# Attention by groups of four heads over all queries, and the MLP at the end: reordering a tuned transformer-block kernel

## The chip, the cores and the metric

The kernel runs on one core of one Trainium2 chip. The metric is the device time of one execution in microseconds (us). A run is called slow if it is over 1.5% above the fastest of the same kernel; all comparisons below use fast runs only. Profiles are of one execution each.

Engines are named as in the profile: PE is TensorE (matmul), PEld its weight load (it overlaps PE), ACT is ScalarE, DVE is VectorE, POOL is GpSimd, SP is SyncE, whose queue (SPq) only issues DMAs here. SBUF and PSUM are the two memories in which the kernel keeps its tiles; it has matmuls write their results to PSUM. "L657" is line 657 of the kernel in question; line numbers of different kernels are not comparable.

## The reference

A block on 2048 tokens of width 640: attention of 32 heads (width 128) against a given cache of 2048 keys and values, then an MLP with a token shift. Both branches are modulated and gated by vectors computed from `c`.

```python
mod = (_silu(c) @ w_mod)                      # six vectors: sa ca ga sb cb gb
h = _layernorm(x) * (1 + ca) + sa
x = x + ga * attention(h, k_cache, v_cache, wq, wo)   # q = h @ wq, softmax over 2048 keys, @ wo
h = _layernorm(x) * (1 + cb) + sb
# _B_ref(h):
g  = _gelu(_layernorm(h) @ w1)                # 640 -> 640; quarters shifted by +1, -1, +2, -2 tokens
x1 = h + shifted(g) @ w2                      # 640 -> 640
h2 = _gelu(_layernorm(x1) @ w3) @ w4          # 640 -> 1728 -> 640
x = x + gb * (x1 + h2)
```

## The kernel before

Both kernels record all work as operations with a *planned* duration, a priority and the tiles read and written. A small list scheduler in the kernel simulates the engines with these durations and so fixes, before anything runs, the order of instructions of each engine. Semaphore waits follow from the tiles. A planned duration costs nothing on the chip, but it decides what stands behind what in an engine's queue.

```python
# choice of the scheduler in before: of what can start within 30 ns, the lowest priority number
    lim = min(st)[0] + 30.0
    c = min((x for x in st if x[0] <= lim), key=lambda x: x[1:3])
```

Before works chunk by chunk. For each of four chunks of 512 queries it runs through all 32 heads, so a *step* is one chunk and one head, and there are 128 steps. K, V and the query weights are loaded anew in each step.

```python
def step(ch, h):                              # s = ch * 32 + h
    dma("SP", ... e.dma_start_transpose(k.ap..., A_k_cache[0, h]) ...)     # K transposed by DMA
    dma("POOL", ... A_wq[:, h*128:(h+1)*128] ...)
    dma("POOL", ... A_v_cache[0, h] ...)
    P.op("PE", qp, KT * MM(QC), ...)          # query projection: 5 matmuls of 512 columns
    for j in range(NKT // 2):                 # 8 slots a step, each of 256 keys
        P.op("PE", smm, 2 * MM(QC), ..., s + j / 8 - 1.0)           # scores: 2 matmuls of 512 columns
        last_exp[s, j] = P.op("ACT", ... ACT.Exp ..., 1040, (sp,), (pt,), s + j / 8, ...)
        for b in range(2):
            P.op("PE", pv, 4 * 59, (pt, v), (o[b],), s + j / 8 - 0.9 + b * 0.01, accum=True)  # values
    # ... divide by the row sums on DVE into On
def wo_group(ch, g): ...                      # after each 4 heads: transpose On by DMA, project, add to y
def phase_b(ch): ...                          # MLP of chunk ch, run during the heads of chunk ch + 1
```

The elementwise work ahead of the MLP is all on DVE, two fused instructions a tile for the modulation; the inverse standard deviation comes from two tiny ACT instructions (Ln, then Exp with scale -0.5):

```python
    P.op("DVE", ... e.scalar_tensor_tensor(out=w.ap, in0=src, scalar=mvt[:, 0:1], in1=mod_t[pc][:],
                                           op0=ALU.subtract, op1=ALU.mult) ...)
    P.op("DVE", ... e.scalar_tensor_tensor(out=dst, in0=w.ap, scalar=rst.ap, in1=mod_t[pb][:],
                                           op0=ALU.mult, op1=ALU.add) ...)
```

Of the kernel before, what the change touches and what calls it, by code (L numbers as in the profile page):

```python
# [7 lines left out]
ACT = mybir.ActivationFunctionType  # L8
# [5 lines left out]
class Op:  # L14

    def __init__(self, eng, fn, dur, lat, prio, dma, kb):
        self.eng, self.fn, self.dur, self.lat, self.prio, self.dma, self.kb = eng, fn, dur, lat, prio, dma, kb
        self.deps = {}
        self.order = set()
        self.newps = None  # L20
        self.ptiles = ()
        self.succ = []
        self.ready = 0.0
        self.needed = False
        self.sem = self.semval = self.prev_dma = None
# [15 lines left out]
class Plan:  # L41
# [5 lines left out]
    def __init__(self):  # L47
        self.ops = []
        self.pools = {}

    def op(self, eng, fn, dur, reads=(), writes=(), prio=0.0, lat=80, dma=False, kb=0, after=(), accum=False):
        o = Op(eng, fn, dur, lat, prio, dma, kb)
# [23 lines left out]
        o.order.update(after)  # L76
        self.ops.append(o)
        return o

    def schedule(self):  # L80
        for o in self.ops:
            o.order = {d() if callable(d) else d for d in o.order}
            pre = set(o.deps) | o.order
            for d in pre:
                d.succ.append(o)
            o.ndep = len(pre)
# [7 lines left out]
        free = {p: [(0.0, b, ()) for b in range(len(bk))] for p, bk in self.pools.items()}  # L94
        left = {o.newps: len(o.newps.refs) for o in self.ops if o.newps is not None}
        self.busy = {e: 0.0 for e in self.ENG}
        self.all = []
        while len(self.all) < len(self.ops):
            best = None
            for e in self.ENG:  # L100
                st = []
                for o in avail[e]:
                    r = o.ready
# [10 lines left out]
                if best is None or c[0] < best[0]:  # L114
                    best = c
            s, o = best[0], best[3]
            e = o.eng
            avail[e].remove(o)
            if o.newps is not None:
# [16 lines left out]
            self.all.append(o)  # L136
            for u in o.succ:
# [14 lines left out]
    def emit(self, nc, es, ndma):  # L152
# [21 lines left out]
        for o in self.ops:  # L174
            for d, raw in o.deps.items():
                if waits_on(o, d, raw):
                    d.needed = True
# [9 lines left out]
        for o in self.all:  # L187
            kn = know[o.eng]
            w = {}
            ds = [d for d, raw in o.deps.items() if waits_on(o, d, raw)]  # L190
# [42 lines left out]


def fast_path(nc, es, flag, A_x, A_k_cache, A_v_cache, A_wq, A_wo, B_w1, B_w2, B_w3, B_w4, c, w_mod, out):
# [6 lines left out]
    FL = FF - (NF - 1) * 128  # L242
    G4 = D // 4
    HG = 4
    SCALE = float(DH) ** -0.5
# [8 lines left out]
    T = lambda ap: Tile(ap)  # L254

    def ring(name, n, shape, dt):
        return [T(sb("%s%d" % (name, i), shape, dt)[:]) for i in range(n)]

    S_ps = [ps("S%d" % i, [128, 1024]) for i in range(2)]
    O_ps = [ps("O%d" % i, [128, 512]) for i in range(2)]  # L260
    M_ps = [ps("M%d" % i, [128, 512]) for i in range(2)]
    P.pools = {"S": [t[:] for t in S_ps], "O0": [O_ps[0][:]], "O1": [O_ps[1][:]], "M": [t[:] for t in M_ps]}

    ident_t = sb("ident", [128, 128], BF16)
    ident = T(ident_t[:])
    ones = T(sb("ones", [128, 128], BF16)[:])
    mod = [[T(None), T(None)] for _ in range(6)]
    mod_t = [sb("mod%d" % i, [128, D], F32) for i in range(6)]
    rl_t = sb("rl", [128, 4 * NC * H], F32)
    rl = T(rl_t[:])  # L270
    WA_t = sb("WA", [128, NF * D], BF16)
    WB_t = sb("WB", [128, KT * FF], BF16)
    WA, WB = T(WA_t[:]), T(WB_t[:])
    small = lambda name, w, dt=F32: T(sb(name, [128, w], dt)[:])

    MM = lambda n: n / 2.4 + 3
    dve = lambda n, psum=False: (n + (150 if psum else 90)) / 0.96
    act = lambda n: (n + 230) / 1.2

    def dma(eng, fn, kb, reads, writes, prio):  # L280
        return P.op(eng, fn, 60 if eng == "SP" else 1000, reads, writes, prio, dma=True, kb=kb)

    P.op("POOL", lambda e: e.memset(ident_t[:], 0.0), 200, (), (ident,), -100)
    P.op("POOL", lambda e: e.affine_select(out=ident_t[:], in_=ident_t[:], pattern=[[-1, 128]], compare_op=ALU.not_equal,
                                           fill=1.0, base=0, channel_multiplier=1), 300, (ident,), (ident,), -100)
    P.op("POOL", lambda e: e.memset(ones.ap, 1.0), 200, (), (ones,), -50)

    EXPSET = "natural_log_exp_and_others"
    P.op("ACT", lambda e: e.preload_act_table_set(EXPSET), 1300, (), (), -200)

    def back_to_exp(g, prio):
        o = P.op("ACT", lambda e: e.preload_act_table_set(EXPSET), 1300, (), (), prio, after=tuple(g))
        return (o,)

    c_sb, c_e, c_f = small("c_sb", KT, BF16), small("c_e", KT), small("c_f", KT)
    s_bc = T(sb("s_bc", [128, KT, 128], BF16)[:])

    def ld_c(e):
        with nc.allow_non_contiguous_dma(reason="tiny c vector"):
            return e.dma_start(c_sb.ap, c[0].rearrange("(kt p) -> p kt", p=128))  # L300
    dma("SP", ld_c, 2, (), (c_sb,), -100)

    xin = ring("xin", 3, [128, D], BF16)
    n_x = [0]

    def load_x(j, prio):
        t = xin[n_x[0] % 3]
        n_x[0] += 1
        dma("SP", lambda e: e.dma_start(t.ap, x2d[j * 128:(j + 1) * 128, :]), 160, (), (t,), prio)
        return t  # L310

    first_x = [load_x(j, -99 + j) for j in range(2)]

    P.op("ACT", lambda e: e.activation(c_e.ap, c_sb.ap, ACT.Exp, scale=-1.0), 300, (c_sb,), (c_e,), -90)
    P.op("DVE", lambda e: e.tensor_scalar_add(out=c_e.ap, in0=c_e.ap, scalar1=1.0), 100, (c_e,), (c_e,), -90)
    P.op("DVE", lambda e: e.reciprocal(c_e.ap, c_e.ap), 150, (c_e,), (c_e,), -90)
    P.op("DVE", lambda e: e.tensor_mul(out=c_f.ap, in0=c_e.ap, in1=c_sb.ap), 100, (c_e, c_sb), (c_f,), -90)
    P.op("DVE", lambda e: e.tensor_copy(s_bc.ap, c_f.ap.unsqueeze(2).to_broadcast([128, KT, 128])), 700, (c_f,), (s_bc,), -90)

    def mod_part(p, stage, prio):  # L320
        st_t = (WA_t, WB_t)[stage]
        stt = (WA, WB)[stage]
        wv = st_t[:, 0:KT * D].rearrange("p (k n) -> p k n", k=KT)
        dma("SP", lambda e: e.dma_start(wv, w_mod[:, p * D:(p + 1) * D].rearrange("(k p) n -> p k n", p=128)), 800, (), (stt,), prio)
        for hf in range(2):
            m = Tile(pool="M")
            sl = slice(hf * HD, (hf + 1) * HD)

            def mm(e, m=m, sl=sl):
                for k in range(KT):  # L330
                    ins = e.matmul(m[:, 0:HD], s_bc[:, k, :], wv[:, k, sl], start=(k == 0), stop=(k == KT - 1))
                return ins
            P.op("PE", mm, KT * MM(HD), (s_bc, stt), (m,), prio)
            P.op("DVE", lambda e, m=m, sl=sl: e.tensor_scalar_add(out=mod_t[p][:, sl], in0=m[:, 0:HD],
                                                                 scalar1=1.0 if p in (1, 4) else 0.0),
                 dve(HD, True), (m,), (mod[p][hf],), prio - 5)

    SA, CA, GA, SB, CB, GB = range(6)
    mod_part(CA, 0, -98.5)
    mod_part(SA, 1, -98)  # L340

    NS = 3
    st = [small("st%d" % i, 12) for i in range(NS)]
    mv = [small("mv%d" % i, 2) for i in range(NS)]
    rs = [small("rs%d" % i, 1) for i in range(NS)]
    n_st = [0]

    def ln(src, src_tiles, prio):
        i = n_st[0] % NS
        n_st[0] += 1  # L350
        for hf in range(2):
# [1060 lines left out]
```

## Time and profile before

| before | |
|---|---|
| time, median of 3 runs | 1687.13 us (1683.19 to 1698.67) |
| span of the profiled run, mean granted clock | 1689.8 us, 0.953 |
| start of the first exponential / of the last one | 44.50 / 1569.20 us |
| PE busy / ACT busy | 87% / 69% |
| DMA traffic | 239.20 MB |

The profile page, the busy times and some rows of the span cut in 40 slices. A digit is the busy share of a slice in tenths, and PEclk is the granted TensorE clock in tenths.

```profile
PE 1467.7 (87%) x13043; PEld 914.0 (54%) x13043; DVE 574.6 (34%) x1334; ACT 1162.1 (69%) x1330; POOL 308.6 (18%) x322
...
PE   3999999999699997999698997899969899899357
...
PEclk9999999999799998999799998999979999999789
...
DMA packets 412920, 239.20 MB, mean 142 GB/s; under 512 B 371888, under 2 KB 381872, under 8 KB 412784
```

PE is nearly full, with dips: at the very start, three times in the middle where the clock drops too, and for the last three slices. The next view says what an undisturbed stretch looks like. It is the busy time in windows; columns are the window, its length, then busy us and (instructions) of each engine, then granted clock, DMA share and GB/s.

```profile
200.00:240.00 40.00, 38.35 (x374) 25.02 (x372) 11.16 (x28) 31.14 (x33) 8.89 (x9) 1.00 0.70 157
...
400.00:440.00 40.00, 30.72 (x260) 16.37 (x258) 13.98 (x32) 34.48 (x41) 5.73 (x6) 0.91 0.72 138
440.00:480.00 40.00, 31.49 (x240) 17.58 (x239) 10.70 (x27) 32.85 (x35) 3.93 (x4) 0.79 0.26 61
...
1570.00:1610.00 40.00, 11.73 (x56) 5.64 (x56) 28.30 (x62) 7.08 (x22) 0.00 (x0) 0.66 0.16 34
```

At 200 us PE is busy 38.35 of 40 us. From 400 to 480 us, where the MLP of the first chunk is filled in, PE stands idle for 17.8 us of 80 although ACT is busier than at 200 us. After the last exponential (1570 us on) PE works 11.73 of 40 us at a clock of 0.66.

Why ACT is busy without moving PE is seen on its timeline inside the fill-in. Columns: start, duration, engine, line, operation, output<-input; in brackets the idle time before it and what ended it.

```profile
425.95 1.28 ACT L569 ACT_TABLE_LOAD   x1
427.25 0.60 ACT L569 ACTIVATE f_us<-f_M 128x512 bf16<-128x512 f32 x1
429.19 0.59 ACT L569 ACTIVATE f_us<-f_M 32x512 bf16<-32x512 f32 x1 [1.35 <-PE f_M L565]
429.79 1.28 ACT L461 ACT_TABLE_LOAD   x1
431.08 1.02 ACT L461 ACTIVATE f_PT<-f_S 128x1024 bf16<-128x1024 f32 x1
```

One GELU (L569), one exponential (L461), and a table load of 1.28 us before each. The groups by form count 66 loads of this length, about 85 us.

The pace is best read from the starts of every eighth exponential in the trace, which is the length of a step. Some of the 127 steps of before, in us:

```text
steps 16-23   9.88  9.31 10.64 10.07  9.88  9.31 10.64 10.07     (undisturbed)
steps 36-39   9.55 14.67 31.93 12.84                             (MLP fill-in)
```

### The profile page before, as it was taken

The numbers are of one execution on the slowest core, as the hardware profiler recorded it, in microseconds if no ns is written. First come the engines' busy times: TensorE is split into PE (matmuls) and PEld (weight loads), VectorE is DVE, ScalarE is ACT, GpSimd is POOL, SyncE is SP. The second block draws the span as 40 slices with busy tenths as digits, with TensorE's granted clock in tenths as the row PEclk, the third lists the DMA queues.
The fourth block names the chain that finished last, engine by engine and source line by source line (L and its number), as shares of the span: only waits on it lengthen the run. The fifth ranks groups of instructions, "written<-read, shape, count | busy, mean of one in ns | idle before, by whom it ended". The sixth has DMA issues, their size and how long they took to land.

```text
span 1689.8 us, 30083 instructions
## 1 busy us (share of the span) xinstructions
PE 1467.7 (87%) x13043; PEld 914.0 (54%) x13043; DVE 574.6 (34%) x1334; ACT 1162.1 (69%) x1330; POOL 308.6 (18%) x322
## 2 busy tenths in 40 slices
PE   3999999999699997999698997899969899899357
PEld 1566666666265564666264564566526556566124
DVE  4422222237151242227151234233715123222623
ACT  1687777778967675778976664677886666478261
POOL 2222222222021221222012112222202111211000
PEclk9999999999799998999799998999979999999789
DMA  8967777679286779678468569776819746976120
GB/s 240 219 144 153 155 156 154 149 148 184 48 198 124 172 163 151 148 156 175 83 145 156 139 116 169 150 155 154 181 38 185 129 137 128 168 136 132 32 70 21
DMA packets 412920, 239.20 MB, mean 142 GB/s; under 512 B 371888, under 2 KB 381872, under 8 KB 412784
## 3 DMA queue, kind: packets, MB, share of 16 engines
q1 hardware_dynamic: 376944, 103.92, 37.4%
q0 software_dynamic: 35840, 133.32, 30.1%
q8 instruction: 104, 1.70, 0.4%
q14 instruction: 32, 0.26, 0.1%
HBM read 143.46 MB, written 2.62 MB: 86 GB/s over the span
## 4 chain that ended last, share of the span: by engine, by line
PE 68%; ACT 17%; DMA 7%; DVE 4%; issue 2%; SPq 1%
PE f_O L470 25%; PE f_S L458 20%; ACT f_PT L461 12%; PE f_M L446 8%; PE f_M L501 7%; PE f_M L630 4%; PE f_M L610 3%; DMA f_OT<-f_On 3%; DMA f_KTs<-in_A_k_cache_dram 2%; ACT L569 2%; ACT L461 2%; SPq L439 1%; ACT f_us L569 1%; PE f_M L585 1%; DMA f_nT<-f_nrm 1%
## 5 line engine op out<-in xcount | busy, mean ns | idle before, releaser
L461 ACT ACTIVATE f_PT<-f_S 128x1024 bf16<-128x1024 f32 x1024 | 1000.1, 1021 | 388.3 <-PE f_S L458 384.6
L470 PEld LDWEIGHTS f_O<-f_V,f_PT 128*128 128x128 bf16 x8192 | 514.9, 98 | 297.9 <-ACT f_PT L461 197.0
L470 PE MATMUL f_O<-f_V,f_PT 128*128 128x129 bf16 x8192 | 625.4, 221 | 55.8 <-ACT f_PT L461 45.8
L458 PE MATMUL f_S<-f_QT,f_KTs 128*128 128x512 bf16 x2048 | 593.9, 385 | 57.0 <-ACT f_PT L461 40.7
L441 POOL DMA_DIRECT2D f_V<-in_A_v_cache_dram x128 | 149.6, 1169 | 666.2 <-PE f_O L470 420.8
L449 DVE CAST f_QT<-f_M 128x512 bf16<-128x512 f32 x128 | 88.3, 690 | 531.5 <-PE f_S L458 523.5
L458 PEld LDWEIGHTS f_S<-f_QT,f_KTs 128*128 128x128 bf16 x2048 | 164.0, 97 | 118.6 <-ACT f_PT L461 64.4
L501 PE MATMUL f_M<-f_wo,f_OT 128*128 128x320 bf16 x1024 | 182.8, 306 | 12.4 <-DMA f_OT<-f_On 9.4
L509 DVE TENSOR_TENSOR f_yacc<-f_M,f_yacc 128x320 f32<-128x320 f32 x224 | 109.3, 489 | 246.0 <-PE f_M L501 244.8
L440 POOL DMA_DIRECT2D f_wq<-in_A_wq_dram x128 | 110.9, 867 | 396.6 <-PE f_O L470 349.8
L446 PE MATMUL f_M<-f_hT,f_wq 128*128 128x512 bf16 x640 | 163.0, 387 | 2.2 <-ACT f_hT L394 0.8
L501 PEld LDWEIGHTS f_M<-f_wo,f_OT 128*128 128x128 bf16 x1024 | 97.7, 100 | 83.9 <-DMA f_OT<-f_On 11.1
L481 DVE TENSOR_TENSOR f_On<-f_O,f_rl 128x256 bf16<-128x256 f32 x256 | 107.9, 422 | 7.5
L446 PEld LDWEIGHTS f_M<-f_hT,f_wq 128*128 128x128 bf16 x640 | 62.4, 99 | 80.8 <-issue 6.5
L479 DVE RECIPROCAL f_rl<-f_O 128x2 f32<-128x2 f32 x256 | 42.6, 166 | 116.4 <-PE f_O L470 112.6
L610 PE MATMUL f_M<-f_nT,f_WB 128*128 128x512 bf16 (+5 forms) x350 | 64.0, 343 | 16.3 <-DMA f_nT<-f_nrm 14.0
L630 PE MATMUL f_M<-f_WA,f_gT 128*128 128x320 bf16 x448 | 68.9, 300 | 1.6 <-DVE f_QT L449 1.1
L565 PE MATMUL f_M<-f_nT,f_WA 128*128 128x512 bf16 x100 | 35.6, 509 | 33.7 <-DMA f_nT<-f_nrm 23.6
L630 PEld LDWEIGHTS f_M<-f_WA,f_gT 128*128 128x128 bf16 x448 | 42.5, 97 | 30.9 <-issue 8.4
L610 PEld LDWEIGHTS f_M<-f_nT,f_WB 128*128 128x128 bf16 (+1 forms) x350 | 32.3, 100 | 46.8 <-DMA f_nT<-f_nrm 14.3
L614 ACT ACTIVATE f_gT<-f_M 128x512 bf16<-128x512 f32 (+3 forms) x70 | 35.5, 511 | 31.4 <-PE f_M L610 31.3
L355 ACT ACTIVATE f_rs<-f_mv 128x1 f32<-128x1 f32 x64 | 12.1, 201 | 52.3 <-DVE f_mv L354 51.9
(83 smaller groups left out, 507.8 us busy)
## 6 DMA issues: line engine op xcount, KB each, us to landing
f_V<-in_A_v_cache_dram POOLq DMA_DIRECT2D x128, 512.0 KB, 6.2
f_wq<-in_A_wq_dram POOLq DMA_DIRECT2D x128, 160.0 KB, 4.8
f_wo<-in_A_wo_dram POOLq DMA_DIRECT2D x32, 640.0 KB, 6.2
f_WB<-in_B_w_dram POOLq DMA_DIRECT2D x4, 2160.0 KB, 9.5
f_WA<-in_B_w_dram POOLq DMA_DIRECT2D x4, 2080.0 KB, 10.5
f_WA<-in_B_w_dram POOLq DMA_DIRECT2D x8, 800.0 KB, 14.1
f_xin<-in_A_x_dram SPq DMA_DIRECT2D x32, 160.0 KB, 4.0
out_dram<-f_ob SPq DMA_DIRECT2D x16, 160.0 KB, 1.8
```

Source lines behind the costliest of these rows:

```text
L440: dma("POOL", lambda e: e.dma_start(w.ap, A_wq[:, h * 128:(h + 1) * 128].rearrange("(k p) d -> p k d", p=128)), 160, (), (w,), lp - 0.5)
L441: dma("POOL", lambda e: e.dma_start(v[:, :, 0:128], A_v_cache[0, h].rearrange("(t p) d -> p t d", p=128)), 512, (), (v,), lp + 0.2)
L446: ins = e.matmul(m.ap, w[:, kk, :], hT_t[ch % 2][:, kk, :], start=(kk == 0), stop=(kk == KT - 1))
L449: P.op("DVE", lambda e: e.tensor_copy(q.ap, m.ap), dve(QC, True), (m,), (q,), s - 4)
L458: ins = e.matmul(sp[:, r * QC:(r + 1) * QC], k[:, kt * 128:(kt + 1) * 128], q.ap, start=True, stop=True)
L461: last_exp[s, j] = P.op("ACT", lambda e, sp=sp, pt=pt: e.activation(pt.ap.rearrange("p k q -> p (k q)"), sp.ap, ACT.Exp, scale=SCALE), 104 ...
L470: ins = e.matmul(o[b][:, u * 129:u * 129 + 129], pt[:, r, qt * 128:(qt + 1) * 128], v[:, kt, 0:129], start=(kt == 0 and u == 0), stop=(kt ...
L481: P.op("DVE", lambda e, ov=ov, i0=i0, b=b: e.tensor_tensor(out=On_t[gs][:, 2 * b:2 * b + 2, hh, :], in0=ov[:, 0:258].rearrange("p (u d) -> ...
L501: ins = e.matmul(m[:, 0:HD], OT_t[gs][:, qt, hh, :], w[:, hh, sl], start=(hh == 0), stop=(hh == HG - 1))
L509: P.op("DVE", lambda e, m=m, qt=qt, sl=sl: e.tensor_tensor(out=y_t[:, qt, sl], in0=m[:, 0:HD], in1=y_t[:, qt, sl], op=ALU.add), dve(HD, Tr ...
L610: ins = e.matmul(m[0:fs[f], 0:n], w3v[:, kk, f * 128:f * 128 + fs[f]], nT_t[:, kk, r0:r1], start=(kk == 0), stop=(kk == KT - 1))
L630: ins = e.matmul(m[:, 0:HD], gT_t[0:fs[f], f, i * 128:(i + 1) * 128], w4v[0:fs[f], f, sl], start=(f == 0), stop=(f == NF - 1))
```

## The change

The loops are turned round. For each group of four heads, all four chunks of queries are done before the next group, so K and V of a head are loaded once and kept (five buffers). The output projections are summed in SBUF for all 2048 tokens. The MLP of all chunks follows when attention is over, so that ACT needs the GELU table once. PE gets a strict order: the scheduler may only take the next matmul by key. The keys put scores of slot n at n, the values of a slot three slots later, and spread the query and output projections over the slots. The elementwise work ahead of the MLP goes to POOL, all but half of chunk 2's, and three unfused instructions replace the two fused ones; for chunks 0 to 2 it is to be hidden under the last group, while the last chunk's stands inside the MLP. The inverse standard deviation is computed by ten or so tiny DVE instructions (Newton steps) where ACT is busy with GELU.

The diff, cut to its core (cuts marked with `[...]`; some long lines are broken):

```diff
@@ schedule
+        pe = sorted((o for o in self.ops if o.eng == "PE"), key=lambda o: (o.prio, o.seq))
+        pe_i = 0
 [...]
                 for o in avail[e]:
+                    if e == "PE" and o is not pe[pe_i]:
+                        continue
@@ [...] the step; s is now group, chunk, head
+    def load_head(h):                        # called once per head
+        load_k(h, pr, need=from_slot(n))
+        load_v(h, pr + 1, need=from_slot(n + 2))
 [...]
+    PV_SLOTS = [2, 2, 3, 2, 2, 3, 2]
 [...]
+            for r in range(2):
+                P.op("PE", ... MM(QC), (K[b][kt // 4], q), (sp,), n + 0.01 * r, accum=True)      # scores
 [...]
+                key = NP * s + 3 + slot + 0.3 + 0.01 * (u - acc)                                  # values
+                    kb = key + 0.004 * bk if u < NKT - 2 else NP * s + 9.35 + 0.02 * bk + 0.001 * u
@@ [...] elementwise work ahead of the MLP
+    def mlp_in(ch, prio):
+        rst = rstd_dve if ch == NC - 1 else rstd_act
+        def side(i, fn, n_pool, n_dve, rd, wr):
+            if ch != 2 or i % 2 == 0:
+                pool(fn, n_pool, rd, wr, prio)
+            else:
+                P.op("DVE", fn, n_dve, rd, wr, prio)
 [...]
+                side(i, ... e.tensor_scalar(out=w.ap, in0=x1[t].ap, scalar1=mv..., scalar2=rs...,
+                                            op0=ALU.subtract, op1=ALU.mult), 750, 430, ...)       # L719
+                side(i, ... e.tensor_tensor(out=w.ap, in0=w.ap, in1=mod_t[4][:], op=ALU.mult), 1500, 825, ...)
+                side(i, ... e.tensor_tensor(out=xb[t].ap, in0=w.ap, in1=mod_t[3][:], op=ALU.add), 1500, 825, ...)
+            rst(g2, a, a + 2, prio)
+                side(i, ... e.tensor_scalar(out=xn[i].ap, in0=xb[t].ap, ...), 750, 430, ...)      # L729
@@ [...] after w2 of a pair of tiles
+                if t < SQ // 128 - 4:
+                    pool(... e.tensor_tensor(out=v.ap, in0=v.ap, in1=mod_t[5][:], op=ALU.mult), 1500, ...)  # L822
+                    pool(... e.tensor_tensor(out=v.ap, in0=v.ap, in1=x1[u].ap, op=ALU.add), 1500, ...)      # L823
@@ [...] order of the MLP: A = w1 of a chunk, B = w2 of a tile, C = w3, D = w4, I = mlp_in, WO = last projection
+    plan = ("A0 A1 B0 B1 B2 B3 WO I3 A2 B4 B5 B6 C0 B7 D0 D1 D2 D3 C1 A3 B8 B9 B10 B11 D4 D5 D6 D7 "
+            "B12 B13 B14 B15 C2 D8 D9 D10 D11 C3 D12 D13 D14 D15").split()
```

## The prediction

> **What bounds the kernel now.** TensorE (PE), on 87% of the span (busy table) and 68% of the chain that ended last; ACT is next with 69%. I cost PE from gapless bursts in the timeline: a pair of 512-column score matmuls advances it 0.43 us, eight 129-column value matmuls 0.46, a query projection 1.08, four output-projection matmuls 0.54. The Trainium skill ("TensorE: Matmul & The Clock Gate", "Wait — 56ns, not 53.3ns?") gives columns at 2.4 GHz plus about 2.5 ns; 57.5 ns for 129 columns and 215 for 512 agree.
>
> A head-and-chunk step therefore needs 16x0.215 + 64x0.0575 + 1.08 + 8x0.135 = 9.28 us, 128 steps 1188 us. The MLP has 389,120 columns, about 165 us, the modulation vectors 8. Sum 1361 of the 1690 us span. The other 330 us are waits:
> - Start: the first exponential begins at 44.5 us (timeline), behind a DMA queue issuing K transposes from 3.3 to 25.2 us.
> - Undisturbed attention (windows, 200 to 318.6 us): 9.88 us a step at clock 1.00, 0.6 us too long: PE waits for exponentials (chain of waits). About 77 us if in all steps.
> - MLP between chunks: near 426 us ACT alternates one GELU and one exponential with a 1.28 us table load before each; about 65 loads cost 86 us (groups by form). PE's clock falls to 0.79 at 440–480.
> - DMA pile-ups afterwards, OT transposes taking 16 us to issue, PE stalled (near 640, 900, 1034, 1302, 1442 us).
> - Tail: last exponential ends at 1570, kernel at 1690. PE works 22 of the first 67 us, at clock 0.72.
>
> **What the change does.** It removes hardly any PE work; it removes waits. K and V load once instead of four times (traffic 239 MB to about 80); the table switches once; value matmuls trail their exponential by three slots. Projections are spread so that a slot is 0.89 to 1.8 us of PE work. An exponential costs 0.97 to 1.02 us, 8.0 us a step against 9.28, and S(n+2) needs it about 1.7 us after S(n) starts, against at least 1.8 us of PE work. So PE should run without a gap: 9.3 to 9.45 us a step. Added: MLP elementwise work on POOL (hidden under attention) and Newton steps on DVE (12 operations of about 0.17 us per tile pair). In the MLP, DVE needs about 3.7 us per w2 tile (0.83 add, 2x0.48 statistics, 0.2, about 1.0 Newton, 0.77 normalise) against 1.36 on PE; interleaving covers most, I allow 4–5 us stall in two places.
>
> **Sum (estimates from these durations).** First scores at 19 us; attention 128x9.33 = 1194; modulation inside it 5; handover (last values, GELU table) 4; MLP and last output projection 170; MLP stalls 10; output 4: 1406 us. All of it lies on the PE critical path.
>
> Predicted **1406 us**, 8 in 10 within **1375 to 1450**. Faster by over 2%: 0.97; within 2%: 0.02; slower: 0.01.
>
> **What would show it.** PE busy share over 93%, mean clock about 0.98; first exponential before 25 us; steps of 9.3 to 9.5 us in windows across the middle, almost no PE wait on ACT; two GELU/exponential table loads, not some 65; DMA share under 0.4 in the middle; from last exponential to end 180 to 195 us.
>
> **What would make it wrong.** Strict PE order turns any late input into a stall nothing can fill: output transposes behind K pieces on the one SP queue (deadline about 10 us after the step; 5.9 us median landing, 20.9 at worst); K/V of heads 1 to 3 late in the first 30 us; w2 tiles that wait for DVE. Each microsecond per step would add 128 us.

## The result, and the profile after

The changed kernel takes 1462.01 us (median of 4 runs, 1461.42 to 1463.73), against 1690.08 us of before in the same rounds (4 runs). The ratio is 0.8652, with a 95% interval of 0.8602 to 0.8701. A ratio here is from the fast runs of both kernels in the same rounds, so it is not quite the ratio of the medians quoted. The direction was right and most of the gain came, but the time lies 12 us above the range of the prediction and 56 us above its centre.

The same rows of the page, after.

```profile
PE 1398.9 (96%) x13079; PEld 942.3 (65%) x13079; DVE 549.8 (38%) x1371; ACT 1097.6 (75%) x1165; POOL 195.3 (13%) x122
...
PE   8999999999999999999999999999999888877997
...
POOL 0000000000000000000000000000002988478300
...
DMA packets 259625, 88.89 MB, mean 61 GB/s; under 512 B 237280, under 2 KB 258208, under 8 KB 259488
```

PE is full until slice 31 of 40, and from there on it reads 8 and 7. POOL, which had nothing to do until then, works there, at 7 to 9 tenths in most slices. The windows (same columns as before) show the same by numbers.

```profile
600.00:640.00 40.00, 40.00 (x407) 28.05 (x405) 11.45 (x28) 35.02 (x36) 0.00 (x0) 1.00 0.45 90
...
1120.00:1160.00 40.00, 36.18 (x343) 24.48 (x342) 16.32 (x45) 29.66 (x37) 31.20 (x18) 0.96 0.21 39
1160.00:1200.00 40.00, 34.71 (x330) 23.39 (x327) 15.44 (x44) 26.76 (x33) 37.20 (x22) 0.96 0.16 32
1200.00:1240.00 40.00, 33.22 (x301) 22.39 (x302) 25.16 (x59) 26.92 (x36) 31.84 (x17) 0.91 0.39 107
1240.00:1280.00 40.00, 31.58 (x167) 16.71 (x165) 26.14 (x65) 22.59 (x34) 18.52 (x13) 0.91 0.29 61
1280.00:1320.00 40.00, 29.80 (x147) 14.66 (x147) 33.60 (x102) 8.35 (x14) 32.28 (x21) 0.87 0.11 23
```

In the middle PE is busy 40.00 of 40 us. From about 1103 us (step 116, in the last group of heads) and in the first part of the MLP it loses 4 to 10 us in each 40.

The steps, from the starts of every eighth exponential:

```text
steps 20-115   9.26 each                                              (predicted: 9.28 of work, 9.33 allowed)
steps 116-126  9.53 10.48 10.11 10.85 11.56 11.62 13.42 10.87 11.81 12.43 10.93
```

The span divides into three parts, by the first and the last exponential's start:

| us | before | after | difference |
|---|---|---|---|
| start to first exponential | 44.50 | 21.02 | -23.5 |
| first to last exponential | 1524.70 | 1217.23 | -307.5 |
| last exponential's start to the end | 120.6 | 222.5 | +101.9 |
| span | 1689.8 | 1460.7 | -229.1 |

The middle and the end must be read together, since the MLP of three of the four chunks moved from the one to the other. After's MLP is 172.3 us of PE work, so about 129 us changed place (an estimate, three quarters of it). Of the 307.5 us that the middle lost, 129 are therefore moved work and some 178 are waits and slowed work that are gone. The end took on 129 us of work and grew by only 101.9, so it wastes about 27 us less than before's. The traces agree: over the whole span the time in which no matmul is recorded fell from 222.1 to 61.8 us, and the time in which PE worked at a granted clock of 0.5 from 81.3 to 45.0 us.

So what of the remaining 55 us between 1460.7 and 1406? Set against the terms of the prediction:

| term (us) | predicted | measured | miss |
|---|---|---|---|
| to the first scores | 19 | 19.95 | +1 |
| first scores to the end of the last exponential | 1194 + 5 | 1219.3 | +20.3 |
| of which steps 116 to 126 above 9.26 us | 0 | 21.8 | +21.8 |
| of which modulation vectors (steps 17 to 19 above 9.26) | 5 | 8.6 | +3.6 |
| of which all other steps | 1194 | 1189 | -5 |
| from there to the end | 188 | 221.4 | +33.4 |
| of which PE work at clock 1.00 (MLP 172.3, last projection 4.35) | 170 | 176.7 | +6.7 |
| of which last matmul to the end | 4 | 8.9 | +4.9 |
| of which PE waits and slowed PE work (the rest) | 14 | 35.8 | +21.8 |

The PE work is an estimate from the distances between matmul starts where the clock is 1.00. Two terms carry nearly all of the miss, each 21.8 us: the last group of heads, and the rest in the MLP. Neither is waiting alone. In the MLP PE has no matmul on record for 25.6 us of the 35.8, and works for 17.2 us at a granted clock of 0.5, which cost about 8.6 (an estimate, half of it). In steps 116 to 126 it is idle for 12.6 us and works for 10.2 us at a clock of 0.5, about 5.1 lost; the other 4 us are longer busy time, of which 2.3 (steps 116 to 118) are the same in every run but pv_lag1 and pv_lag2. The list of waits for the first (engine, line, what it waited for: us in total, times, longest), for 1120 to 1240 us:

```profile
PE f_S L657 <- ACT f_PQ L659: 11.0, 7, 2.8
PE f_O L676 <- DVE f_OO L685: 3.1, 2, 2.4
```

Scores wait for exponentials. But the exponentials are not slower there (1.01 us for the one below), and ACT is busy less, 26.76 us of 40 at 1160 us against 35.02. The timeline around one such wait shows what ACT was doing: nothing.

```profile
1139.21 0.89 DVE L460 BATCH_NORM_STATS2 f_small<-f_y 128x6 f32<-128x320 f32 x2 [2.37 <-POOL f_y L723]
...
1141.93 0.20 ACT L465 ACTIVATE f_small<-f_small 128x2 f32<-128x2 f32 x1 [2.50 <-DVE f_small L461]
1142.05 1.01 ACT L659 ACTIVATE f_PQ<-f_S 128x1024 bf16<-128x1024 f32 x1
...
1143.11 0.60 PE L657 MATMUL f_S<-f_PQ,f_KV 128*128 128x512 bf16 x2 [2.34 <-ACT f_PQ L659]
```

ACT sat idle for 2.50 us before a Ln of 0.20 us (L465). That Ln needs statistics from DVE, which need a tile from POOL that came late. The exponential for which PE was waiting stood behind the Ln. The Trainium skill ("TensorE: Matmul & The Clock Gate", "Architectural detail: the array is 16× 32×32, not 1× 128×128") says that ACT and DVE are strict first-in-first-out queues; the trace agrees: the exponential of 1142.05, whose scores were done at 1139.42, did not begin before the Ln did, 2.6 us late.

POOL's durations, from the groups by form (busy us, mean ns of one, idle before):

```profile
L719 POOL TENSOR_SCALAR f_tmp<-f_hT,f_small 128x640 f32<-128x640 bf16 x14 | 36.3, 2603 | 19.1 <-ACT f_small L466 16.2 <-DVE f_small L475 2.9
L729 POOL TENSOR_SCALAR f_xn<-f_y,f_small 128x640 bf16<-128x640 f32 x14 | 36.1, 2589 | 13.4 <-ACT f_small L466 9.1 <-DVE f_small L481 4.3
L722 POOL TENSOR_TENSOR f_tmp<-f_tmp,f_mod 128x640 f32<-128x640 f32 x14 | 22.2, 1606 | 0.1
```

The `tensor_scalar`, planned with 750 ns, takes 2.6 us. A pair of tiles costs POOL about 24 us: the chain that ended last has a first L719 at 1129.69, at 1153.85, at 1178.13 and at 1202.29 us, with POOL in most of the time between.

In the MLP the largest wait is of w2's matmuls (L805) for DVE, which adds their results (L808) and so frees their PSUM buffer. The list of waits from 1240 us to the end, its first lines:

```profile
PE f_M L805 <- DVE f_y L808: 8.4, 2, 8.0
PE f_O L787 <- DMA f_nTx<-f_xn: 4.1, 1, 4.1
PE f_M L846 <- DVE f_wo L850: 3.7, 1, 3.7
PE f_S L787 <- ACT f_PQ L791: 3.3, 2, 2.2
```

DVE's timeline ahead of that 8.0 us wait; POOL began L822 at 1275.86 us and ended L823 at 1281.91:

```profile
1274.77 0.15 DVE L480 TENSOR_TENSOR f_small<-f_small 128x2 f32<-128x2 f32 x1
...
1276.22 1.52 DVE L480 TENSOR_TENSOR f_small<-f_small 128x2 f32<-128x2 f32 x1
1277.66 0.48 DVE L460 BATCH_NORM_STATS2 f_small<-f_hT 128x6 f32<-128x320 bf16 x1
1278.07 1.16 DVE L481 SCALAR_TENSOR_TENSOR f_small<-f_small 128x2 f32<-128x2 f32 x1
...
1283.37 0.61 DVE L484 TENSOR_SCALAR f_xn<-f_y,f_small 128x640 bf16<-128x640 f32 x1
...
1283.96 0.82 DVE L808 TENSOR_TENSOR f_y<-f_M,f_y 128x640 f32<-128x640 f32 x1
1284.70 1.25 DVE L484 TENSOR_SCALAR f_xn<-f_y,f_small 128x640 bf16<-128x640 f32 x1
```

A Newton step on two numbers a partition takes 0.15 us when POOL is idle and 1.52 us when POOL is in a `tensor_tensor`. The statistics in between, with one input, keep their 0.48 us. The Trainium skill ("SBUF — State Buffer", "Who interferes with whom") says that DVE and GpSimd share a port pair under an exclusive lock, and that a DVE instruction with two SBUF inputs contends with a GpSimd instruction that reads SBUF. These lines fit that: the two-input forms are stretched to about one POOL instruction, the statistics aren't. But not every form with one tensor input is spared: the normalising L484 took 0.61 us with POOL idle and 1.25 us with POOL in L822 (begun at 1284.06 us).

### The profile page after: what moved, and what is told of

Read it like the earlier page. It is cut to its first block, busy times and chain, and to the rows that moved or that the text cites. A ratio compares the mean times of both kernels' runs of the same rounds, so it can differ in the third digit from the quotient of the medians.

```text
span 1460.7 us, 29783 instructions
## 1 busy us (share of the span) xinstructions
PE 1398.9 (96%) x13079; PEld 942.3 (65%) x13079; DVE 549.8 (38%) x1371; ACT 1097.6 (75%) x1165; POOL 195.3 (13%) x122
## 2 busy tenths in 40 slices
DMA packets 259625, 88.89 MB, mean 61 GB/s; under 512 B 237280, under 2 KB 258208, under 8 KB 259488
## 4 chain that ended last, share of the span: by engine, by line
PE 83%; POOL 8%; DVE 5%; ACT 2%; DMA 1%; issue 1%; SPq 0%; ACTq 0%; POOLq 0%
PE f_O L676 29%; PE f_S L657 28%; PE f_M L600 9%; PE f_M L627 9%; POOL f_tmp L719 2%; PE f_M L846 2%; PE f_S L846 2%; POOL f_xn L729 2%; POOL f_tmp L722 1%; DVE f_small L460 1%; PE f_O L833 1%; PE f_S L833 1%; POOL f_y L723 1%; ACT f_PQ L659 1%; DMA f_xin<-in_A_x_dram 1%
## 5 line engine op out<-in xcount | busy, mean ns | idle before, releaser
L659 ACT ACTIVATE f_PQ<-f_S 128x1024 bf16<-128x1024 f32 x1024 | 1030.6, 1022 | 172.1 <-PE f_S L657 168.9
L676 PEld LDWEIGHTS f_O<-f_KV,f_PQ 128*128 128x128 bf16 x8192 | 542.5, 98 | 218.9 <-DVE f_OO L685 4.3
L657 PE MATMUL f_S<-f_PQ,f_KV 128*128 128x512 bf16 x2048 | 613.5, 381 | 12.9 <-ACT f_PQ L659 11.2
L676 PE MATMUL f_O<-f_KV,f_PQ 128*128 128x129 bf16 x8192 | 616.3, 220 | 5.6 <-DVE f_OO L685 3.1
L634 DVE TENSOR_TENSOR f_y<-f_M,f_y 128x320 f32<-128x320 f32 x216 | 105.5, 489 | 561.2 <-PE f_M L627 561.2
L627 PE MATMUL f_M<-f_wo,f_OO 128*128 128x320 bf16 x992 | 270.5, 299 | 0.0
L657 PEld LDWEIGHTS f_S<-f_PQ,f_KV 128*128 128x128 bf16 x2048 | 192.8, 98 | 58.0 <-ACT f_PQ L659 14.5
L627 PEld LDWEIGHTS f_M<-f_wo,f_OO 128*128 128x128 bf16 x992 | 95.0, 98 | 27.9
L603 DVE CAST f_PQ<-f_M 128x512 bf16<-128x512 f32 x128 | 88.4, 691 | 61.5 <-PE f_M L600 61.5
L685 DVE TENSOR_TENSOR f_OO<-f_O,f_rl 128x256 bf16<-128x256 f32 x256 | 108.3, 423 | 8.3
L460 DVE BATCH_NORM_STATS2 f_small<-f_y 128x6 f32<-128x320 f32 x64 | 29.5, 481 | 25.6 <-POOL f_y L723 25.4
L719 POOL TENSOR_SCALAR f_tmp<-f_hT,f_small 128x640 f32<-128x640 bf16 x14 | 36.3, 2603 | 19.1 <-ACT f_small L466 16.2
```

The lines of the kernel that those rows point to most:

```text
L460: P.op("DVE", lambda e, hf=hf: e.bn_stats(s[:, hf * 6:hf * 6 + 6], src[:, hf * HD:(hf + 1) * HD]), 485, src_t, (s,), prio)
L603: P.op("DVE", lambda e: e.tensor_copy(q.ap, m.ap), 690, (m,), (q,), s * NP - 90)
L627: P.op("PE", lambda e, m=m, qt=qt, hf=hf, hh=hh: e.matmul(m[:, 0:HD], OT_ap[gs][:, qt, hh, :], wo_t[g % 2][:, hh, hf * HD:(hf + 1) * HD], ...
L634: x = P.op("DVE", lambda e, m=m, yt=yt: e.tensor_tensor(out=yt.ap, in0=m[:, 0:HD], in1=yt.ap, op=ALU.add), 490, (m, yt), (yt,), s * NP - 60)
L657: P.op("PE", lambda e, sp=sp, r=r, kt=kt: e.matmul(sp[:, r * QC:(r + 1) * QC], K_ap[b][:, kt * 128:(kt + 1) * 128], q.ap, start=True, stop ...
L659: x = P.op("ACT", lambda e, sp=sp, pt=pt: e.activation(pt.ap.rearrange("p k q -> p (k q)"), sp.ap, ACT.Exp, scale=SCALE), 1021, (sp,), (pt ...
```

## The experiments

The expectations use letters for the theories:

- **A**: the plan believes in 0.75 us for POOL's `tensor_scalar`, so it puts ACT's small Ln and Exp too early in ACT's queue, and exponentials wait behind them.
- **B**: POOL's `tensor_tensor` holds the port that DVE's two-input instructions need, so DVE's small steps in the MLP are stretched.
- **C**: POOL's chain is simply too slow. Whatever the order, its results come too late for the MLP.
- **D**, a rival for the MLP: DVE has too much work of its own there, whatever POOL does.

Kernels ran against the kernel before in the same rounds. Ratios are to before; the changed kernel's is 0.8652. Each experiment starts from the changed kernel. All results were correct. The changed kernel itself was not run again beside them, and before's median moved from 1687.03 to 1690.08 us, so a difference of 3 us from the changed kernel says nothing by itself.

### plan_pool_times: tell the plan the truth, change no instruction

```diff
-                     750, 430, (x1[t], mvs[g1][i], rs[g1]), (w,))
+                     2600, 840, (x1[t], mvs[g1][i], rs[g1]), (w,))
 [...]
-                     750, 430, (xb[t], mvs[g2][i], rs[g2]), (xn[i],))
+                     2600, 610, (xb[t], mvs[g2][i], rs[g2]), (xn[i],))
```

> Only two planned durations change: the scale-and-shift instructions on POOL are planned at 2.6 us (as the trace has them) in place of 0.75. No instruction changes, only the fixed order of each queue. Theory A (ACT executes in order; the small Ln/Exp of the layer norms were planned among the exponentials for a POOL result that arrives late, so the exponentials behind them wait, and PE with them): the excess of the last group's steps over 9.26 us falls from 22 us to under 8, the MLP phase hardly changes, total 1444 to 1454. Theory B (the VectorE/POOL port lock delays the query casts and evacuations in the last group): within 3 us of 1462. Theory C (POOL is simply too slow, whatever the order): within 3 us of 1462.

Measured: 1457.11 us (1455.09 to 1459.07), ratio 0.8648 (0.8586 to 0.8710). The last exponential starts at 1213.55 us, 25 us earlier than in the changed kernel, and the scores' waits for ACT in the last group fall from 11.0 to 0.2 us. The total falls by 5, between the ranges expected for A and for C. Its waits, from 1200 us to the end:

```profile
PE f_S L787 <- DMA f_wo<-f_xn: 13.4, 1, 13.4
PE f_O L787 <- DMA f_wq<-f_xn: 10.6, 1, 10.6
```

w1's matmuls (L787) now wait 24 us for normalised tiles. So A is right about where the waits in attention come from, but what it saves there is paid a little later. This run is the reason not to call A the cause of the time.

It does not show C cleanly either. The new order puts more of the small Ln and Exp among the GELUs: the trace has 19 table loads in place of 6, and from 1216 to 1268 us POOL itself is idle for 14.8 us, waiting for ACT's Exp (L466):

```profile
1251.51 1.28 ACT L466 ACT_TABLE_LOAD   x1
...
1253.11 2.84 POOL L719 TENSOR_SCALAR f_tmp<-f_hT,f_small 128x640 f32<-128x640 bf16 x1 [7.03 <-ACT f_small L466]
```

How much of the 24 us is POOL's slowness and how much ACT's switching is not taken apart here. That POOL's slow instructions cost time rests on ts_on_dve and stt_mix.

### ts_on_dve: the two slow instructions to DVE

```diff
-                side(i, lambda e, ...: e.tensor_scalar(out=w.ap, in0=x1[t].ap, ...), 750, 430, ...)
+                ts(lambda e, ...: e.tensor_scalar(out=w.ap, in0=x1[t].ap, ...), 840, ...)          # P.op("DVE", ...)
 [...]
-                side(i, lambda e, ...: e.tensor_scalar(out=xn[i].ap, in0=xb[t].ap, ...), 750, 430, ...)
+                ts(lambda e, ...: e.tensor_scalar(out=xn[i].ap, in0=xb[t].ap, ...), 610, ...)
```

> The two POOL scale-and-shift instructions of a tile (2.6 us each) go to DVE (about 0.84 and 0.61). Theories A and C: the POOL chain of a tile pair shrinks from 24 to about 14 us, the last group's excess falls below 8 us, the MLP input of the last chunk is ready some 18 us earlier, so that the 4.1 us wait for it goes; total 1430 to 1442. Theory B: small DVE instructions stay stretched (means 0.27 to 0.30 us in the Newton steps), the 8 us wait of the w2 tile on DVE stays, total 1450 to 1460.

Measured: 1439.94 us (1438.31 to 1441.08), ratio 0.8547 (0.8486 to 0.8607), so 22 us less than the changed kernel. The last exponential starts at 1221.8 us, 16 us earlier, and nothing is paid back behind it. The last group's excess falls from 21.8 to 5.7 us and the 4.1 us wait for the last chunk's input goes, as A and C expected. The 8.0 us wait of w2 stays, as it should if it has another cause.

### no_pool: all elementwise work of the MLP on DVE

```diff
-            if ch != 2 or i % 2 == 0:
+            if False:
                 pool(fn, n_pool, rd, wr, prio)
 [...]
-                if t < SQ // 128 - 4:
+                if False:
                     pool(... mod_t[5] ...)
```

(with the DVE durations 840 and 610 planned.)

> All elementwise work of the MLP goes from POOL to DVE: no POOL lateness, no port lock. Theories A, B and C: Newton instructions at 0.15 to 0.17 us in place of 0.27 to 0.30, the last group's excess under 4 us; total 1420 to 1436. Rival D (DVE's own amount of work holds the w2 tiles up, POOL was a help): the last group improves but the MLP phase from last exponential to end, now 221 us, stays or grows because DVE gets some 40 us more work there; total 1445 or more.

Measured: 1459.93 us (1457.96 to 1460.75), ratio 0.8659 (0.8597 to 0.8721): no gain. The two halves cancel. The last exponential starts at 1220.8 us and L480 never takes more than 163 ns (its median is 153), so the stretching goes away with POOL, as B says. The last group's excess is 6.5 us (under 4 were expected). But DVE's own work now stands in the way (D); its waits from 1240 us:

```profile
PE f_S L846 <- DVE f_small L480: 15.0, 1, 15.0
PE f_M L805 <- DVE f_y L808: 14.7, 3, 10.3
```

POOL must carry a part, only not these parts.

### rstd_dve: no Ln and Exp on ACT for the MLP

```diff
-        rst = rstd_dve if ch == NC - 1 else rstd_act
+        rst = rstd_dve
```

> The inverse root of the layer norms in the MLP input is taken on DVE (Newton) for all chunks, as it is for the last one, so ACT has nothing that depends on POOL. Theory A: waits of scores on exponentials in the last group (11 us) vanish and so do the four extra table loads just after the last exponential; last group's excess under 8 us; total 1438 to 1448. Theory B: DVE gets 12 more small instructions a tile pair beside a busy POOL, each stretched, so evacuations and casts are late and the excess stays above 15 us; total within 5 us of 1462.

Measured: 1469.40 us (1466.44 to 1471.02), ratio 0.8719 (0.8656 to 0.8782), slower than the changed kernel. The scores' waits for ACT vanish (0.2 us), and so do the extra table loads at the handover. But DVE is a queue too. It now waits for POOL with its Newton steps, and PE waits for DVE instead: L676 for DVE 12.3 us in the last group, with steps of 16.22, 14.95 and 13.52 us, and L787 10.8 us in the MLP. Moving the victim of a late input to another in-order engine does not make the input earlier. This fits C. B had also expected an excess above 15 us here (it is 20.6), but of the 81 small two-input DVE instructions in the last group only 3 took over 0.4 us, so stretching is not what costs it.

### pad_w4: the last block of w4 padded from 64 rows to 128

In the changed kernel a w4 tile, 28 matmuls, takes 4.22 us, that is 151 ns each, where 320 columns had been costed at 135. Its block of 64 rows was suspected.

```diff
+    P.op("DVE", lambda e: e.memset(w4_ap[NF - 1][FL:128, :], 0.0), 200, ...)
+                P.op("DVE", lambda e: e.memset(gT_ap[FL:128, NF - 1, :], 0.0), 200, ...)
 [...]
-                fs = FS[f]
+                fs = 128
```

> The last of the 14 row blocks of the w4 product has 64 rows; here its weights and activations are padded with zeros to 128, so that every matmul of the product uses the full array. Theory E (the matmul beside a change of row count costs more, so that a w4 tile of 28 matmuls takes 4.22 us where 28 x 0.136 would be 3.81): a tile takes 3.8 us, 16 tiles save 6 to 7 us where PE is the limit (the last 100 us), total 1455 to 1458. Rival (0.151 us a matmul has another cause, e.g. the gaps of the weight loads): tile unchanged at 4.2 us, total within 2 us of 1462.

Measured: 1457.75 us (1457.02 to 1458.72, 6 runs), ratio 0.8655 (0.8616 to 0.8694). The tile, from PE's timeline of the changed kernel:

```profile
1434.88 4.29 PE L846 MATMUL f_M<-f_KV,f_OO 128*128 128x320 bf16 x28
1439.11 4.29 PE L846 MATMUL f_S<-f_KV,f_OO 128*128 128x320 bf16 x28
```

and of pad_w4:

```profile
1435.64 3.97 PE L849 MATMUL f_S<-f_KV,f_OO 128*128 128x320 bf16 x28
1439.45 3.97 PE L849 MATMUL f_M<-f_KV,f_OO 128*128 128x320 bf16 x28
```

Start to start it is 4.23 us against 3.81: 28 x 135 ns is 3.78. The suspicion is right in the tile, 0.42 us of 16 tiles each, 6.7 us. Of that 4.3 us arrive in the total; its list of waits has longer ones instead (w1 for its tiles 5.7 us against 4.1, and w4 for a GELU 3.8 us).

### pv_lag1 and pv_lag2: values one or two slots after their exponential's slot, not three

```diff
-                key = NP * s + 3 + slot + 0.3 + 0.01 * (u - acc)
+                key = NP * s + 1 + slot + 0.3 + 0.01 * (u - acc)            # pv_lag2: + 2
 [...]
-                    kb = ... NP * s + 9.35 + ...
+                    kb = ... NP * s + 7.35 + ...                            # pv_lag2: 8.35
```

> Value matmuls trail the exponential of their tile by one slot in place of three, all else equal. Theory F (the lag is what took the 0.6 us of waits per step away): PE waits again for the exponential in most slots, steps of 9.7 to 10.1 us in place of 9.26, total 1515 to 1560. Rival (the steps of before were long because of its DMA traffic and fill-in work, not the lag): steps within 0.1 us of 9.26, total within 15 us of 1462.

> Value matmuls trail by two slots, between the 3 of the changed kernel (9.26 us a step) and the 1 that gave 15 to 16 us. By the changed kernel's own times an exponential ends 1.66 us after its score pair starts, and the value matmuls of the slot after the next start 1.3 to 1.5 us after it where three half-tiles are packed into one slot: a wait of 0.2 to 0.4 us twice a step, steps of 9.3 to 9.9 us, total 1465 to 1545. If the lag acts gradually (one slot of lag worth 3 us a step): 11 us or more a step, over 1680.

Measured: pv_lag1 2292.75 us (2291.02 to 2300.27), ratio 1.3622 (1.3539 to 1.3705); pv_lag2 1514.43 us (1513.31 to 1516.49), ratio 0.8985 (0.8942 to 0.9028). Steps in the middle are 15.3 to 16.3 us and 9.61 us, against 9.26.

The direction is as expected, and for two slots the size too. For one slot the size is far off: 6 to 7 us more a step, not under 1. The list of waits of pv_lag1 over the whole span begins with

```profile
PE f_O L676 <- ACT f_PQ L659: 619.6, 733, 3.5
```

What I had overlooked is in the code: the packs of values are [2, 2, 3, 2, 2, 3, 2], so some of a slot's values reach a slot ahead, and with a lag of one they follow the scores of their *own* slot. In a strict order score, exponential and value then run one after the other, and PE waits 5.7 times a step (733 waits in 128 steps). This reading rests on the code and the list of waits; no run tests the packs alone. In pv_lag2 the expected wait twice a step is not seen: the list names 1.8 us of waits for exponentials in all, and the 0.35 us a step are made up of matmuls that start up to 0.2 us late (read from one step of the trace). Both runs together show that, under the strict order, the step of 9.26 us rests on the lag of three. They do not separate the strict order from the lag; the next one does so for the lag of three only.

### free_order: same keys, but the scheduler may take any matmul that is ready

```diff
-                    if e == "PE" and o is not pe[pe_i]:
+                    if False:
                         continue
```

> The same keys, but PE takes whatever the planner thinks can start first, as the kernel before did, in place of the strict order. If the strict order itself is worth something: the steps lengthen by 0.1 us or more, 1475 to 1530. If the keys (lag and spread) are what counts: attention steps within 0.1 us of 9.26; the MLP phase, where strict order had 25 us of waits, may lose up to 20 of them: 1440 to 1465.

Measured: 1451.29 us (1450.85 to 1452.05), ratio 0.8617 (0.8566 to 0.8668), 11 us *less* than the changed kernel. In the middle the steps are 9.26 us just the same; the steps of the modulation vectors are shorter (11.03, 11.98, 10.21 us against 11.98, 13.56, 10.84), and the last exponential starts at 1230.1 us, 8 us earlier (3.2 of them from the modulation steps, 3.2 from the first 17 steps). With the lag of three the strict order is by itself worth nothing; it costs 11 us. A short lag without strict order was not run. Before comes near it: its values have a priority less than a slot behind their scores, PE takes what is ready, and its undisturbed steps are 9.3 to 10.6 us, not the 15 to 16 of pv_lag1.

### stt_mix: fused modulation back on DVE, POOL keeps two instructions a tile

```diff
-            if ch != 2 or i % 2 == 0:
+            if True:
                 pool(fn, n_pool, rd, wr, prio)          # only y * GA and + x are left here
 [...]
-                side(... tensor_scalar ...); side(... tensor_tensor mult ...); side(... tensor_tensor add ...)
+                P.op("DVE", ... e.scalar_tensor_tensor(out=w.ap, in0=x1[t].ap, scalar=mv..., in1=mod_t[4][:], ...), 880, ...)
+                P.op("DVE", ... e.scalar_tensor_tensor(out=xb[t].ap, in0=w.ap, scalar=rs..., in1=mod_t[3][:], ...), 880, ...)
 [...]
-                side(... tensor_scalar(out=xn[i].ap ...), 750, 430, ...)
+                P.op("DVE", ... e.tensor_scalar(out=xn[i].ap, ...), 610, ...)
```

> MLP input with the modulation fused into two DVE instructions (subtract-multiply, multiply-add; 0.88 us each in the trace of before) and the last normalisation on DVE; POOL keeps only the first multiply and add of a tile (3 us a tile in place of 11). Theories A and C (POOL's lateness is the cause): last group's excess under 6 us, no wait for the MLP input of the last chunk, total 1420 to 1436. Rival D (DVE's queue is the limit in the MLP): MLP phase still has 20 us or more of PE waits on DVE results, total 1437 to 1455.

Measured: 1435.08 us (1433.40 to 1436.75), ratio 0.8523 (0.8472 to 0.8574), 27 us less than the changed kernel. Steps 119 to 126 are back to 8.2 to 10.4 us, much as in plan_pool_times, but here the tiles are ready in time as well. A and C's expectations are met (excess 3.8 us, no wait for the last chunk's input). D is not far off either: PE still waits 17.9 us for DVE in the MLP, 12.8 of them in one wait of w2.

### late_gb: the end of a tile moved from POOL to DVE

POOL's L822 and L823 compute h·gb + x ahead of time, so that the last step of a tile is shorter. Without them DVE does three instructions at the end of a tile in place of two (in the last four tiles, whose h·gb + x was on DVE before, three in place of four). POOL keeps the input work of the last chunk in the MLP (its L719 begins at 1284.96 us here).

```diff
-                    pool(... in0=v.ap, in1=mod_t[5][:], op=ALU.mult ...); pool(... in1=x1[u].ap, op=ALU.add ...)
 [...]
-        P.op("DVE", ... out=two(w.ap), in0=wide(m), in1=two(mod_t[5][:]), op=ALU.mult ...)
-        P.op("DVE", ... out=o_.ap, in0=w.ap, in1=b.ap, op=ALU.add ...)
+        P.op("DVE", ... out=two(w.ap), in0=wide(m), in1=two(b.ap), op=ALU.add ...)
+        P.op("DVE", ... out=w.ap, in0=w.ap, in1=mod_t[5][:], op=ALU.mult ...)
+        P.op("DVE", ... out=o_.ap, in0=w.ap, in1=x1[t].ap, op=ALU.add ...)
```

> The last multiply and add of a tile go back to where the w4 result is read (three DVE instructions a w4 tile, as in the kernel before) and leave POOL, where they ran beside the layer norms of the w2 tiles. Theory B (the shared port: small two-input DVE instructions wait for the POOL instruction in progress, 1.0 to 1.5 us each, inside the 8.0 us wait of the fifth w2 tile): that wait shrinks to 4 us or less, the Newton instructions average under 0.24 us, total 1444 to 1455; the last group is as in the changed kernel (excess about 22 us). Rival D (amount and order of DVE work alone): the 8 us wait stays within 1.5 us, total 1458 or more because the final tiles get 0.8 us more DVE work.

Measured: 1447.01 us (1446.68 to 1447.52), ratio 0.8583 (0.8543 to 0.8623), 15 us less, although DVE has 8 instructions more (1379; its busy time falls from 549.8 to 536.6 us). The same place of DVE's timeline as above, which runs alike up to 1276.20 us:

```profile
1276.20 0.15 DVE L480 TENSOR_TENSOR f_small<-f_small 128x2 f32<-128x2 f32 x1
...
1279.52 0.82 DVE L808 TENSOR_TENSOR f_y<-f_M,f_y 128x640 f32<-128x640 f32 x1
```

L808 comes 4.44 us earlier, and four instructions that had been stretched (1.52, 1.16, 1.02 and 1.31 us, at about 0.15 each now) account for 4.4 us. The wait of w2 falls from 8.0 to 3.6 us. In this stretch DVE has the same instructions in the same order in both kernels, so these 4.4 us are B's. The other 10 of the 15 us are not split: the end of a tile and the planned order of DVE changed too, other waits went with them (w4's for the DVE instruction that reads its result, from 3.7 to 0.2 us), and the time that PE works at a clock of 0.5 in the MLP fell from 17.2 to 8.0 us. The last group of heads is as it was (22 us above 9.26 a step), as it should be.

### combo1 and combo2: the parts together

combo1 is stt_mix, late_gb and pad_w4 in one kernel. It also plans the normalising DVE instruction (L484) with 700 and 440 ns in place of 430 and 240, which none of the three did, so it is not their pure sum. combo2 moves the input work of the last chunk, which is now mostly on DVE, behind the first w2 tiles of chunk 1:

```diff
-    plan = ("A0 A1 B0 B1 B2 B3 WO I3 A2 B4 B5 B6 C0 B7 ...
+    plan = ("A0 A1 B0 B1 B2 B3 WO A2 B4 B5 B6 I3 C0 B7 ...
```

> stt_mix, late_gb and pad_w4 together. If their causes are separate the gains add: from 1435, minus 6.5 for the padding, minus 5 to 15 for the MLP without POOL: 1413 to 1424. If late_gb only moves the wait to another DVE instruction: 1427 to 1432.

> combo1 with the MLP input of the last chunk queued after three w2 tiles in place of before them (it is needed only some 50 us later). If the 12.8 us wait of the fifth w2 tile in stt_mix comes from DVE's order: the wait goes, 1403 to 1415, and at least 6 us below combo1. If it comes from the port alone, which combo1 has already relieved: within 3 us of combo1.

Measured: combo1 1426.69 us (1424.84 to 1428.04), ratio 0.8461 (0.8420 to 0.8501); combo2 1423.29 us (1422.14 to 1426.42), ratio 0.8446 (0.8405 to 0.8488). Single gains of 27, 15 and 4 us would add up to 46; combo1 shows 35, between the two expected ranges and nearer the one in which the wait moves: w2 still waits for DVE (6.9 us), and w4 5.4. In combo2 w2's wait shrinks to 1.1 us, and the time by 3.4 us, not the 6 or more that were expected (the runs of the two overlap, so the size is uncertain). Other waits come in its place:

```profile
PE f_S L828 <- DMA f_wq<-f_xn: 6.1, 1, 6.1
PE f_M L841 <- DVE f_wo L845: 5.0, 1, 5.0
```

combo2 beats both kernels: 39 us under the changed one. Its last exponential ends at 1217.7 us, where the prediction had 1218 (19 + 1194 + 5). From there it takes 203.7 us, the prediction had 188. With these repairs the attention part is as costed, though the agreement to 0.3 us is luck: first scores, modulation and last group are 1.5, 3.6 and 3.8 us over, and the other steps 9.3 us under, because 9.26 us came where 9.33 were allowed. The 16 us that are left lie behind the last exponential.

### All runs at a glance

| kernel | median us | ratio to before |
|---|---|---|
| changed kernel | 1462.01 | 0.8652 |
| plan_pool_times | 1457.11 | 0.8648 |
| ts_on_dve | 1439.94 | 0.8547 |
| no_pool | 1459.93 | 0.8659 |
| rstd_dve | 1469.40 | 0.8719 |
| pad_w4 | 1457.75 | 0.8655 |
| pv_lag1 | 2292.75 | 1.3622 |
| pv_lag2 | 1514.43 | 0.8985 |
| free_order | 1451.29 | 0.8617 |
| stt_mix | 1435.08 | 0.8523 |
| late_gb | 1447.01 | 0.8583 |
| combo1 | 1426.69 | 0.8461 |
| combo2 | 1423.29 | 0.8446 |

The intervals of the ratios are about 0.4 to 0.6 hundredths wide on either side (0.8 for pv_lag1), and the runs of before spread most. The medians of the new kernels are much steadier (the 4 to 6 runs of each lie within 5 us, those of pv_lag1 within 10), so "less than the changed kernel" is read from medians; plan_pool_times, pad_w4 and no_pool, within 5 us of it, are told apart from it by their profiles and not by their ratios.

## Why the prediction was right, and where it was wrong

- **Right: what bounds before.** The gain is mostly waits: of the 229 us of span, 160 are time without a matmul. PE's share of the span went from 87 to 96%, its mean clock from 0.953 to 0.979, traffic from 239.20 to 88.89 MB, and the first exponential from 44.50 to 21.02 us (predicted: over 93%, about 0.98, about 80 MB, before 25 us).
- **Right: the cost of a step.** 9.28 us were summed from matmul durations, 9.26 came, for about 100 steps without a gap. The columns-at-2.4-GHz figure of the Trainium skill, named in the prediction, held in these steps, at clock 1.00 (216 ns from start to start for 512 columns, 57 for 129). That the lag of three slots is needed was argued there; pv_lag1 and pv_lag2 show it for the strict order.
- **Wrong step: "MLP elementwise work on POOL (hidden under attention)".** The prediction gave this work no time and no path to PE. It was not hidden: the last group runs 21.8 us over, and 16 and 18 of them go when the slow instructions leave POOL (5.7 left in ts_on_dve, 3.8 in stt_mix). Its `tensor_scalar` takes 2.6 us, the chain POOL to DVE to ACT holds up exponentials in ACT's queue, and repairing the plan alone pays the lateness in the MLP, in part as table loads (plan_pool_times). The two runs that take the slow instructions off POOL give 22 and 27 us back in all. Before's trace held no POOL instruction of this kind, so there was no duration to cost it with, and I let the plan's 750 ns pass unasked. The Trainium skill ("GPSIMD Engine Reference", "4.1 Engine selection") calls one-input work on GpSimd "roughly line-rate", which the trace contradicts for this form.
- **Mis-sized: the MLP's waits.** The terms "MLP stalls 10" and "handover 4" measured 35.8 together, 25.6 of it waits and most of the rest PE work at a clock of 0.5, for which the prediction had no term. It counted DVE's work with undisturbed durations ("about 1.0 Newton"), and POOL beside it stretched it; late_gb gives 15 us back, of which 4.4 are traced to stretched instructions. no_pool and the combos show the other half: DVE's own work, in its order, is also near its limit there, which "interleaving covers most" understated. At the handover one Ln and one Exp among the GELUs cost four more table loads of 1.28 us (1248.36 to 1254.58 us) and PE two waits for ACT of 2.2 and 2.0 us; the prediction had two loads in all.
- **Mis-sized: PE work at the end, 170 against 176.7,** by the 64-row block (pad_w4: 6.7 us). Before computes the same block, so its trace could have shown it; I took 135 ns from the output projection's matmuls instead.
- **Mis-sized: the tail after the last matmul, 4 against 8.9.** Before's trace has 8.6 at the same place (last matmul to 1681.24, span 1689.8); I didn't look.
- **Named as risks and not seen:** output transposes behind K pieces on the SP queue, and late K and V of heads 1 to 3. In the list of waits of the first 230 us the largest wait for K or V is 2.3 us. The third named risk, w2 tiles that wait for DVE, did come: 8.4 us.
- **Open.** That strict order alone gains nothing with the lag of three is shown, but how the gain in the middle divides between loading K and V once, moving the MLP out, and the keys, was not taken apart. Of the last 16 us behind combo2's last exponential, the tail after the last matmul is 6 (9.8 against 4); for the rest the list of waits says where PE waits, but no run shows the order that would remove them.

## What to carry to other kernels

When work is moved to an idle engine as "hidden", cost it as a chain: its measured duration, who waits for each piece, and what stands behind that waiter in an in-order queue. A planner's duration is a claim; when the trace holds no instance of an instruction, measure one before you trust it, since repairing only the plan moves the wait and not the work. An idle engine is not free for its neighbours either: judge the move by how long the other engine's small instructions take while it runs.

## What the Trainium skill lacked or had wrong

- "GPSIMD Engine Reference", section 4.1, calls 1-input elementwise work "roughly line-rate". A `tensor_scalar` on POOL with one 128x640 tensor input and two per-partition scalars took 2.59 to 2.60 us (14 each of two forms), longer than a two-input `tensor_tensor` of that size (1.40 to 1.66 us). The figure of its section 3.1 for the latter, about 2.6 cycles an element, gives at 1.2 GHz an estimate of 1.39 us and holds for the shortest form.
- "SBUF — State Buffer", "Who interferes with whom", describes the lock rightly, but gives no number for tiny instructions: Newton steps on 128x2 went from 0.15 us to between 1.0 and 1.5 us, and a row of them delayed DVE by 4.4 us.
- "ScalarE: Activation LUTs", "What ACT_TABLE_LOAD costs", says 1283 ns for the load and about 1380 ns of drain, 2.66 us for every switch. The loads here measure 1283 ns, but no drain is seen: one activation ended at 429.78 us, the load began at 429.79 and the next activation at 431.08, so a switch cost 1.30 us.
- "TensorE: Matmul & The Clock Gate", "Why this matters for your kernels", says that a single matmul of few rows takes the time of a full one. Among 128-row blocks of the same accumulation, one block of 64 rows cost 0.21 us a group more than a padded one (4.23 against 3.81 us for a tile of two groups). "TensorEngine Tiling (Array Packing)", "Key Properties", says that changing the tiling mode drains TensorE, without a number; that this is what is paid here is not shown.
